# Seven products for the output stages of three middle blocks, on a ring of 2048 tokens, with other places for the folds

## The chip, the core and the metric

The kernel runs on one core of one Trainium2 chip. Its time is device time in microseconds (us), the median of repeated runs. The core's engines are called PE (TensorE, matmuls; PEld its weight loads), DVE (VectorE), ACT (ScalarE), POOL (GpSimd) and SP (SyncE, which issues DMAs). Each engine runs its own instructions in program order and waits for the others through semaphores.

## What is computed

Two stages follow one another: attention over pooled keys and values, then a feed-forward layer whose hidden value is the largest of three products. Cut to the lines that matter:

```python
# q, k, v: (8 batches, 8 heads, 576 tokens, 64)
k_p = k.reshape(B, H, 72, 8, 64).mean(axis=3)      # every 8 keys into one
v_p = v.reshape(B, H, 72, 8, 64).mean(axis=3)
attn = softmax(q @ k_p.T / sqrt(64))
x = (attn @ v_p).transpose(0, 2, 1, 3).reshape(4608, 512)
h = max(max(x @ w1, x @ w2), x @ w3)               # 512 -> 768
out = h @ w_out                                    # 768 -> 512
```

## The kernel before

**Blocks.** The 4608 tokens are worked through in nine blocks of 512, numbered 0 to 8. A block has a hidden stage (`hidden`, L364) and an output stage (`project`, L382). The attention of the coming batches (576 tokens each, so the borders of batches and blocks don't agree) is woven into the matmuls of these stages by hand: a block's list gives, for a numbered slot in the stream of matmul groups, the steps that are issued there (`block` L499, `plan1` L523, `plan` L533). The steps (`do`, L278) are k (transpose the folded keys into `pkt` and copy them into `kz`: two copies on DVE, two on ACT, L198), q or T (transpose q, on PE or by DMA), s0 to s7 (scores of a head into `psc`, exponential into `et` on ACT), v0 to v4 (values of 128 tokens into `pav`; reciprocal and product `xn` on DVE, L261 and L263), x0 to x4 (transpose `xn` into `xT`, on PE up to batch 2 and by a DMA transpose on SP's queue behind it).

**Hidden stage.** The weights w2 and w3 have w1 subtracted, so that h = x w1 + max(0, x(w2-w1), x(w3-w1)). For each of six column groups jc, one group of four matmuls (L347) gives `pw1`, which ACT turns into `t` (L353), and a second gives `pw2`; DVE writes hT = max(t, pw2) (L355). `pw` has three PSUM buffers. Blocks 0 to 5 do this directly; blocks 6 to 8 (the woven end of the program) use seven products instead of eight (Strassen's scheme, `seven`, L753) for it.

**Output stage.** The part x w1 w_out is taken with a matrix wm = w1 w_out, which block 0 computes (`linear`, L329: four groups of six matmuls L334 into `pw` buffers, copied to `wm` by DVE and ACT in turn, L338). A block's four tiles of 128 tokens each take four matmuls with wm (L392) and six with w_out (L396), 128x512 each, into one PSUM bank, which ACT copies to `osb` (L401) for SP to store. Blocks 7 and 8 do this in seven products as well (`out_seven`, L661): a product is ten 128x256 matmuls (L715). It needs sums of the quarters of [wm; w_out], which POOL makes during the last blocks (`fold_out`, L622, 20 instructions L630), and sums of the quarters of [x, h] (`fold_x`, `fold_h`).

**POOL.** Its queue issues the loads of q, k, v and the weights, and folds the eight keys or values that are averaged: `fold` (L147) is three additions of halves (L151, L152, L154). `pool_work` (L543) puts, at the start of each block, the loads for three batches on, then the folds of two or three tensors. Only batch 1's k is folded by DVE (step K in block 0). Sums of the hidden weights for blocks 6 to 8 (`fold_w`, L572) are DVE work in block 5.

Of the kernel before, what the change touches and what calls it, by code (L numbers as in the profile page):

```python
# [14 lines left out]
def kernel(  # L15
# [129 lines left out]
    xT = const.tile([128, KCH, TOK], F16, name="xT", tag="xT")  # L145

    def fold(e, t, out, dtype=F32):  # L147
        part, n = t.shape[:2]
        f = const.tile([part, n, 4, D], dtype, name="half" if dtype == F32 else "halfh",
                       tag="half" if dtype == F32 else "k16")  # L150
        e.tensor_tensor(out=f, in0=t[:, :, 0:4, :], in1=t[:, :, 4:8, :], op=ALU.add)  # L151
        e.tensor_tensor(out=f[:, :, 0:2, :], in0=f[:, :, 0:2, :], in1=f[:, :, 2:4, :],  # L152
                        op=ALU.add)
        e.tensor_tensor(out=out, in0=f[:, :, 0, :], in1=f[:, :, 1, :], op=ALU.add)  # L154
# [81 lines left out]
    def turn_x(b, c0, keep, xn, tag, evac=nc.scalar.copy):  # L236
        if b > 2:
            g0 = S * b + c0
            nc.sync.dma_start_transpose(
                out=xT[:, :, g0 + keep:g0 + 128],  # L240
                in_=xn.rearrange("p g h d -> p (g h d)")[keep:128])
            return
        pxt = psum([128, KCH, 128], F16, name="pxt", tag=tag[0], bufs=tag[1])
        for kc in range(KCH):
            nc.tensor.transpose(
                pxt[:, kc, :],
                xn[:, kc // 2, 2 * (kc % 2):2 * (kc % 2) + 2, :], identh)
        g0 = S * b + c0
        evac(out=xT[:, :, g0 + keep:g0 + 128], in_=pxt[:, :, keep:128])  # L249
# [28 lines left out]
    def do(b, steps):  # L278
# [3 lines left out]
        for name in steps.split():  # L282
# [16 lines left out]
            elif name[0] == "d":  # L299
                for j in range(2):  # L300
                    sub_w(i, j, j + 1)
            elif name[0] == "z":
# [39 lines left out]
    def hidden_part(n, jc, c0, c1, hT):  # L342
        col = slice(NB * n + c0, NB * n + c1)
        for wi in range(1, 3):
            pw = psum([128, c1 - c0], F32, name=f"pw{wi}", tag="pw", bufs=3)
            for kc in range(KCH):
                mm = nc.tensor.matmul(pw, w_sb[wi][:, kc, bass.ts(jc, 128)],  # L347
                                      xT[:, kc, col],
# [32 lines left out]

    def project(n):  # L382
        hT = hTs[n]
        for mm in range(4):
            m = 4 * n + mm
            last = m == TOK // 128 - 9
            osb = sb3.tile([128, C], F32, name="osb", tag="osb", bufs=5)
            for c in ((slice(0, C // 2), slice(C // 2, C)) if last else (slice(0, C),)):
                tag = PW if len(pools) < 3 else PA if last else PO
                po = psum([128, c.stop - c.start], F32, name="po", tag=tag[0], bufs=tag[1])  # L390
                for kc in range(KCH):
                    nc.tensor.matmul(po, xT[:, kc, bass.ts(m, 128)], wm_sb[:, kc, c],  # L392
                                     start=(kc == 0), stop=False)
# [103 lines left out]
    FOLDS = (2, 3, 4, 5, 6, 7, 8, 10)  # L497

    def block(n, plan, parts, folds=()):  # L499

        for slot, _ in enumerate(part for stage in parts for part in stage(n)):
            if slot == 0 and n > 0:
                pool_work(n, mms[-1])
# [3 lines left out]
            if folds and slot in FOLDS:  # L507
                next(folds.pop(0))

    fold_v(1)  # L510
    block(0, {0: [(0, "v2")], 1: [(0, "v3")], 3: [(0, "x2 x3 w1 v4")], 6: [(0, "x4 d1")], 9: [(0, "w2")], 10: [(0, "d2")], 11: [(0, "w3")], 12: [(0, "w4")], 14: [(0, "w5 z")],
              17: [(1, "K")], 24: [(1, "q0 k")], 25: [(1, "q1")],
              26: [(1, "s0 q2")], 27: [(1, "s1 s2")], 28: [(1, "s3 Q3")],
              29: [(1, "s4 s5")], 30: [(1, "s6 s7")], 31: [(1, "v0")],
              32: [(1, "v1 x0")], 33: [(1, "X1 v2 v3")]}, (hidden, project))
    load_k(3, nc.gpsimd)
    load_v(3, nc.gpsimd)
    load_q(3)
    fold_k(2, nc.gpsimd)
    fold_v(2)  # L520


    def plan1():  # L523
        return {1: [(1, "x2")], 2: [(1, "v4")], 3: [(1, "x3")],
                5: [(1, "x4")],
                6: [(2, "k")], 7: [(2, "q0")], 9: [(2, "q1")], 11: [(2, "q2 s0")],
                12: [(2, "s1 q3")], 13: [(2, "s2")], 14: [(2, "s3")], 15: [(2, "s4"), (3, "T")],
                16: [(2, "s5")], 18: [(2, "s7")],
                19: [(2, "v0")],
                20: [(2, "v1 x0")], 21: [(2, "v2 x1")], 22: [(2, "v3 x2")],  # L530
                23: [(2, "v4 x3")], 24: [(2, "x4"), (4, "T")], 17: [(2, "s6")]}

    def plan(n):  # L533
        b = n + 1
        got = {0: [(b, "k")]}
        got.update({3 + h: [(b, f"s{h}")] for h in range(H)})
        got.update({12 + c: [(b, f"v{c} x{c}")] for c in range(5)})
        got[14 if n == 2 else 13].append((b + 2, "T"))
        return got

    FOLDS_OF = {1: "k3 v3", 2: "k4 v4 k5", 3: "v5 k6 v6", 4: "k7 v7"}

    def pool_work(n, mm):  # L543

        if n + 3 < B:
            if n == 1:
                load_q(4)
            after([load_k(n + 3, nc.gpsimd)], mm)
            load_v(n + 3, nc.gpsimd)
            if n > 1:  # L550
                load_q(n + 3)
        for name in FOLDS_OF.get(n, "").split():
            if name[0] == "k":
                fold_k(int(name[1]), nc.gpsimd)
            else:
                fold_v(int(name[1]))
# [31 lines left out]
    def halves(n):  # L588

        return {i: xT[:, 2 * (i // 2):2 * (i // 2) + 2,  # L590
                      NB * n + HALF * (i % 2):NB * n + HALF * (i % 2) + HALF]
                for i in range(4)}
# [18 lines left out]
    th = {}  # L611

    def out_w(z, r):
# [3 lines left out]
        return wm_sb[:, 2 * j + r, c] if r < 2 else wo_sb[:, JH * j + r - 2, c]  # L617

    def out_s(z):
        return so["S4"][:, 0:5] if z == 4 else so["S123"][:, 5 * z - 5:5 * z]  # L620

    def fold_out():  # L622

        for r in range(5):
            a = [out_w(z, r) for z in range(4)]
            s = [None] + [out_s(z)[:, r] for z in range(1, 5)]
            for out, x, y, op in ((s[1], a[2], a[3], ALU.add), (s[2], s[1], a[0], ALU.subtract),
                                  (s[3], a[0], a[2], ALU.subtract),
                                  (s[4], a[1], s[2], ALU.subtract)):
                after([nc.gpsimd.tensor_tensor(out=out, in0=x, in1=y, op=op)], mms[-1])  # L630
                yield
# [29 lines left out]
    def out_seven(n):  # L661

        o = sb2.tile([128, 2304], F32, name="ob", tag="et")[:, 0:2048].rearrange(
            "p (j m c) -> p j m c", j=2, m=2)
# [3 lines left out]
        def store(e, j, c):  # L668
            for u in range(2):
                b, g = divmod(2 * (4 * n + 2 * j) + u, NG)  # L670
                pair = g + 2 < NG and GS[g + 2] == GS[g] + 4
                for m in range(0, 2, 1 + pair):
# [3 lines left out]
                                in_=o[64 * u:64 * u + 64, j, m:m + 1 + pair, c])  # L676

        def bank(of, m):
            if n < LAST:
                if of not in banks:  # L680
                    if of == "A":
# [13 lines left out]
        def product(i, *ms):  # L695
            for m in ms:
                matmuls(i, m)
# [3 lines left out]
        def matmuls(i, m):  # L701
# [3 lines left out]
            for r in range(5):  # L705
                c = slice(128 * m, 128 * m + 128)
                if isinstance(zb, str):
                    z = int(zb[1]) - 1
                    left = turns(n)[:, z, r, c] if r < 2 else th[n][z][:, r - 2, c]
                else:  # L710
                    at = HALF * (zb % 2) + 128 * m
                    left = (xT[:, 2 * (zb // 2) + r, NB * n + at:NB * n + at + 128] if r < 2
                            else hTs[n][:, JH * (zb // 2) + r - 2, at:at + 128])
                right = out_s(int(za[1]))[:, r] if isinstance(za, str) else out_w(za, r)
# [4 lines left out]
        def evict(i, ms):  # L719
            m, at = ms[0], slice(ms[0], ms[-1] + 1)  # L720

            def copy(j, c):
                nc.scalar.copy(out=o[:, j, at, c], in_=bank("A", m))

            def plus(j, c, of):
                nc.vector.tensor_tensor(out=o[:, j, at, c], in0=o[:, j, at, c],
# [26 lines left out]
    def seven(n):  # L753

        x, banks, done = halves(n), {}, set()
        low = pad[:, 8:10]
# [147 lines left out]
```

## Time and profile before

| | us |
|---|---|
| median of three runs (228.23 to 230.03) | 228.53 |
| span of the profiled execution | 227.0 |
| PE busy in it | 217.5 (96%) |
| POOL busy | 153.5 (68%) |
| DVE busy | 131.5 (58%) |
| ACT busy | 122.1 (54%) |

The page cuts the span into 40 slices, each digit a busy share in tenths:

```profile
PE   7688999999999999999999999999999999999993
...
DVE  3568877038525342634363336388668886798841
...
POOL 7974200999949999999999929930224996994020
PEclk9999999999999999999999999999999999999999
```

PE is full from the third slice to the last but one, and its clock (PEclk) is granted in full throughout. POOL is full from a third to two thirds of the span. In the chain of work that ended last, PE has 70%, DMA 12% and POOL 11% of the span.

In the lines from the trace, the columns are: start in us from the span's start, duration in us, engine, line of the code, operation, output <- inputs, shape, how many instructions are merged, and in brackets the engine's idle time just before and what ended it. In a table by stretch, each engine has its busy time and, in brackets, its number of instructions.

### The profile page before, as it was taken

How to read it: one execution, taken by the hardware profiler on the slowest of the kernel's cores; microseconds unless marked ns; L12 is line 12 of the kernel's file. 1: busy time of each engine (PE TensorE's matmuls, PEld its weight loads, DVE VectorE, ACT ScalarE, POOL GpSimd, SP SyncE). 2: the span in 40 equal slices, each digit the busy share in tenths (PEclk: the TensorE clock that was granted, in tenths of full speed). 3: DMA queues.
4: the chain of work that ended last, by engine and by line, in shares of the span. 5: the costliest groups of instructions: out<-in, count | busy, mean ns of one | idle time of the engine just before them, and what ended most of it. 6: DMA issues, size and time to landing. Idle time of an engine off the chain costs nothing.

```text
span 227.0 us, 4497 instructions
## 1 busy us (share of the span) xinstructions
PE 217.5 (96%) x1716; PEld 137.6 (61%) x1717; DVE 131.5 (58%) x251; ACT 122.1 (54%) x221; POOL 153.5 (68%) x131
## 2 busy tenths in 40 slices
PE   7688999999999999999999999999999999999993
PEld 2377745558656555545554555455677777788882
DVE  3568877038525342634363336388668886798841
ACT  2267524755874578237723872574687446554330
POOL 7974200999949999999999929930224996994020
PEclk9999999999999999999999999999999999999999
DMA  6999999989749999987998699962261544200265
GB/s 160 211 197 197 207 208 208 202 157 229 131 104 183 218 174 210 169 188 131 209 168 196 136 191 185 200 143 56 58 106 36 115 63 90 49 0 0 52 205 164
DMA packets 47413, 33.52 MB, mean 148 GB/s; under 512 B 27104, under 2 KB 42400, under 8 KB 47392
## 3 DMA queue, kind: packets, MB, share of 16 engines
q0 software_dynamic: 16944, 16.98, 46.1%
q1 hardware_dynamic: 30000, 15.87, 32.8%
q10 hardware_dynamic: 448, 0.39, 0.7%
q8 instruction: 13, 0.21, 0.4%
q14 instruction: 8, 0.07, 0.1%
HBM read 34.60 MB, written 9.44 MB: 194 GB/s over the span
## 4 chain that ended last, share of the span: by engine, by line
PE 70%; DMA 12%; POOL 11%; DVE 3%; issue 2%; ACT 0%; POOLq 0%; DVEq 0%; ACTq 0%
PE pw L347 21%; PE po L396 14%; PE po L392 9%; DMA vt<-in_v_dram 8%; PE pA L789 6%; PE psc L207 4%; DMA mw<-in_moe_w_dram 4%; PE pav L255 3%; POOL half L151 3%; PE pC L789 3%; PE oA L715 3%; PE oC L715 2%; POOL half L152 2%; PE pB L789 2%; POOL mw L108 1%
## 5 line engine op out<-in xcount | busy, mean ns | idle before, releaser
L347 PE MATMUL pw<-xT,mw 128*128 128x512 f16 (+1 forms) x336 | 72.8, 348 | 0.3 <-ACT xT L249 0.2
L355 DVE TENSOR_TENSOR hT<-t,pw 128x512 f16<-128x512 f16 (+1 forms) x42 | 25.4, 609 | 34.1 <-ACT et L212 25.9
L347 PEld LDWEIGHTS <-mw 128*128 128x128 f16 x336 | 31.6, 98 | 21.2 <-issue 1.0
L396 PE MATMUL po<-mwo,hT 128*128 128x512 f16 (+1 forms) x174 | 41.0, 371 | 0.0
L212 ACT ACTIVATE et<-psc 72x576 f16<-72x576 f32 (+2 forms) x54 | 35.1, 660 | 6.5 <-PE psc L207 6.4
L151 POOL TENSOR_TENSOR half<-vt 72x2048 f32<-72x2048 f16 x7 | 28.4, 4059 | 14.5 <-DMA vt<-in_v_dram 14.1
L401 ACT COPY osb<-po 128x512 f32<-128x512 f32 (+1 forms) x28 | 16.2, 578 | 35.1 <-PE po L396 31.8
L353 ACT ACTIVATE t<-pw 128x512 f16<-128x512 f32 (+1 forms) x42 | 22.5, 537 | 13.0 <-PE pw L347 11.0
L392 PE MATMUL po<-wm,xT 128*128 128x512 f16 (+1 forms) x116 | 28.9, 371 | 0.1
L263 DVE TENSOR_TENSOR xn<-pav,rcp 128x512 f16<-128x512 f32 x40 | 27.6, 691 | 1.4
L152 POOL TENSOR_TENSOR half<-half 72x1024 f32<-72x1024 f32 (+1 forms) x13 | 27.2, 2095 | 1.0
L396 PEld LDWEIGHTS <-hT 128*128 128x128 f16 x174 | 16.1, 98 | 14.1
L207 PE MATMUL psc<-qT,kz 128*128 128x320 bf16 (+2 forms) x120 | 22.4, 278 | 1.0 <-DVE qT L184 0.9
L151 POOL TENSOR_TENSOR half<-ktFalse 96x1536 f32<-96x1536 f16 x6 | 18.6, 3097 | 4.5 <-DMA ktFalse<-in_k_dram 4.3
L207 PEld LDWEIGHTS <-kz 128*128 128x128 bf16 x143 | 13.1, 98 | 13.3 <-ACT qT L184 1.1
L255 PEld LDWEIGHTS <-et 72*128 72x128 f16 x320 | 15.5, 98 | 7.1 <-issue 0.6
L795 ACT CAST pad<-pA 128x512 f16<-128x512 f32 x27 | 15.5, 587 | 7.2 <-PE pA L789 5.6
L261 DVE RECIPROCAL rcp<-pav 128x8 f32<-128x8 f32 x40 | 8.2, 205 | 19.1 <-PE pav L255 18.8
L255 PE MATMUL pav<-vp,et 72*128 72x65 f16 x320 | 16.9, 194 | 0.3 <-POOL vp L154 0.2
L392 PEld LDWEIGHTS <-xT 128*128 128x128 f16 x116 | 10.5, 98 | 8.2 <-issue 0.2
L769 DVE SCALAR_TENSOR_TENSOR hT<-pad 128x512 f16<-128x512 f16 x18 | 14.4, 812 | 1.7 <-ACT pad L799 1.3
L198 DVE COPY kz<-pkt 64x288 bf16<-64x288 bf16 x18 | 8.7, 481 | 11.5 <-PE pkt L189 11.3
(110 smaller groups left out, 320.2 us busy)
## 6 DMA issues: line engine op xcount, KB each, us to landing
out_dram<-osb SPq DMA_DIRECT2D x54, 128.0 KB, 3.9
ktFalse<-in_k_dram POOLq DMA_DIRECT2D x7, 576.0 KB, 6.6
qb<-in_q_dram POOLq DMA_DIRECT2D x7, 576.0 KB, 13.1
vt<-in_v_dram POOLq DMA_DIRECT2D x7, 576.0 KB, 11.1
mw<-in_moe_w_dram POOLq DMA_DIRECT2D x9, 256.0 KB, 9.4
ktTrue<-in_k_dram SPq DMA_DIRECT2D x3, 384.0 KB, 5.2
out_dram<-ob SPq DMA_DIRECT2D x8, 128.0 KB, 2.6
mwo<-in_moe_w_out_dram POOLq DMA_DIRECT2D x1, 768.0 KB, 13.1
```

Source lines behind the costliest of these rows:

```text
L151: e.tensor_tensor(out=f, in0=t[:, :, 0:4, :], in1=t[:, :, 4:8, :], op=ALU.add)
L152: e.tensor_tensor(out=f[:, :, 0:2, :], in0=f[:, :, 0:2, :], in1=f[:, :, 2:4, :], op=ALU.add)
L207: nc.tensor.matmul(out, kz_all[b % 2][f % 2][:, h, :], qTs[b][:, n + i0:n + i1, 64 * (h % 2):64 * (h % 2) + 64], start=True, stop=True)
L212: nc.scalar.activation(out=out, in_=in_, func=FT.Exp, scale=1.0 / 64.0)
L255: nc.tensor.matmul(pav[:, h // 4, 65 * (h % 4):65 * (h % 4) + 65], ets[b][:, h, c0:c0 + 128], vp_all[:, b, h, :], start=True, stop=True)
L263: nc.vector.tensor_tensor(out=xn, in0=pv[:, :, :, 0:D], in1=rcp.to_broadcast([128, 2, 4, D]), op=ALU.mult)
L347: mm = nc.tensor.matmul(pw, w_sb[wi][:, kc, bass.ts(jc, 128)], xT[:, kc, col], start=(kc == 0), stop=(kc == KCH - 1))
L353: nc.scalar.activation(out=t, in_=pw, func=FT.Relu)
L355: nc.vector.tensor_tensor(out=hT[:, jc, c0:c1], in0=t, in1=pw, op=ALU.max)
L392: nc.tensor.matmul(po, xT[:, kc, bass.ts(m, 128)], wm_sb[:, kc, c], start=(kc == 0), stop=False)
L396: nc.tensor.matmul(po, hT[:, jc, bass.ts(mm, 128)], wo_sb[:, jc, c], start=False, stop=(jc == JCH - 1))
L789: mm = nc.tensor.matmul(p[:, w], a[:, kc, bass.ts(g, 128)], b[:, kc, :], start=(i in FIRST and w + kc == 0), stop=(w + kc == 2), skip_grou ...
```

## The change

- `xT` holds 2048 tokens instead of 4608 and is addressed as a ring (`tokens`). A DMA transpose that crosses the seam is cut in two.
- The output stages of blocks 2, 3 and 4 use `out_seven`: seven products of ten 128x256 matmuls in place of 40 matmuls of 128x512. Product A's results are copied by ACT and products B and C are added by DVE (three additions a block).
- The sums of [wm; w_out] are made early: the rows of w_out by four POOL instructions ahead of POOL's first fold (block 0), the rows of wm by four DVE instructions in block 1 (S). The 20 POOL instructions in the last blocks go.
- Blocks 2 to 4 gain eight DVE sums each: four of tokens (a1 to a4) and four of h (b1 to b4). The weight sums of `fold_w` move from block 5 to blocks 1 to 4 (f).
- The order of blocks 1 to 4 is written as one list (`MIDDLE`), POOL's work included: h is a hidden part, a digit a product of the output stage, F a step of the old output stage, `k5<` a load, `k4+1` one more instruction of the fold of k of batch 4 (`+3`, or `+2` where one is done, ends it). `!` makes POOL's next fold instruction wait for the last sum that DVE was given. In block 2 the step k comes after the second hidden part, in block 4 after the sums a1 to a4.
- `osb` becomes three buffers of two tiles each; the buffers `pad` and `pad4` of the last blocks lie where v and q were loaded.

```diff
-    xT = const.tile([128, KCH, TOK], F16, name="xT", tag="xT")
+    RING = 2048
+    xT = const.tile([128, KCH, RING], F16, name="xT", tag="xT")
+
+    def tokens(t0, t1, k0=0, k1=KCH):
+
+        t0, t1 = t0 % RING, (t1 - 1) % RING + 1
+        assert t0 < t1
+        return xT[:, k0:k1, t0:t1]
...
+        g0 = S * b + c0
         if b > 2:
-            g0 = S * b + c0
-            nc.sync.dma_start_transpose(
-                out=xT[:, :, g0 + keep:g0 + 128],
-                in_=xn.rearrange("p g h d -> p (g h d)")[keep:128])
+            cut = 128 - (g0 + 128) % RING
+            cuts = (keep, cut, 128) if keep < cut < 128 else (keep, 128)
+            for a, z in zip(cuts, cuts[1:]):
+                nc.sync.dma_start_transpose(
+                    out=tokens(g0 + a, g0 + z),
+                    in_=xn.rearrange("p g h d -> p (g h d)")[a:z])
             return
...
+            elif name[0] == "S":
+                next(out_sums, None)
...
-    def plan(n):
-        b = n + 1
-        got = {0: [(b, "k")]}
-        got.update({3 + h: [(b, f"s{h}")] for h in range(H)})
-        got.update({12 + c: [(b, f"v{c} x{c}")] for c in range(5)})
-        got[14 if n == 2 else 13].append((b + 2, "T"))
-        return got
-
-    FOLDS_OF = {1: "k3 v3", 2: "k4 v4 k5", 3: "v5 k6 v6", 4: "k7 v7"}
...
-    def fold_out():
-
-        for r in range(5):
-            a = [out_w(z, r) for z in range(4)]
-            s = [None] + [out_s(z)[:, r] for z in range(1, 5)]
-            for out, x, y, op in ((s[1], a[2], a[3], ALU.add), (s[2], s[1], a[0], ALU.subtract),
-                                  (s[3], a[0], a[2], ALU.subtract),
-                                  (s[4], a[1], s[2], ALU.subtract)):
-                after([nc.gpsimd.tensor_tensor(out=out, in0=x, in1=y, op=op)], mms[-1])
-                yield
+        return so_new[0][:, z - 1]
+
+    def fold_out(e, r0, r1):
+
+        if not so_new:
+            so_new.append(const.tile([128, 4, 5, HALF], F16, name="so", tag="ktTrue"))
+        w = [out_w(z, r0, r1) for z in range(4)]
+        t = [None] + [so_new[0][:, z, r0:r1] for z in range(4)]
+        for out, x, y, op in ((t[1], w[2], w[3], ALU.add), (t[2], t[1], w[0], ALU.subtract),
+                              (t[3], w[0], w[2], ALU.subtract),
+                              (t[4], w[1], t[2], ALU.subtract)):
+            e.tensor_tensor(out=out, in0=x, in1=y, op=op)
+            yield
+
+    out_sums = fold_out(nc.vector, 0, 2)
...
+    def sums_of(n, name):
+
+        t = tt_all[0]
+        h = name[0] == "b"
+        part = t[:, :, 2:5] if h else t[:, :, 0:2]
+        c = ([hTs[n][:, JH * i:JH * i + JH, :] for i in range(2)] if h else
+             [tokens(NB * n, NB * n + NB, 2 * i, 2 * i + 2) for i in range(2)])
+        x = [c[i // 2][:, :, HALF * (i % 2):HALF * (i % 2) + HALF] for i in range(4)]
+        a, b = {"1": (x[1], x[0]), "2": (x[3], part[:, 0]), "3": (x[3], x[1]),
+                "4": (x[2], part[:, 1])}[name[1]]
+        gate[:] = [nc.vector.tensor_tensor(out=part[:, int(name[1]) - 1], in0=a, in1=b,
+                                           op=ALU.subtract)]
...
         def product(i, *ms):
-            for m in ms:
-                matmuls(i, m)
+            if mid:
+                for r in range(5):
+                    for m in ms:
+                        matmuls(i, m, (r,))
+            else:
+                for m in ms:
+                    matmuls(i, m)
             done.update((i, m) for m in ms)
             evict(i, ms)
 
...
+    for _ in fold_out(nc.gpsimd, 2, 5):
+        pass
+    fold_v(1)
...
+    def pool_step(n, name):
+
+        what, b = name[0], int(name[1])
+        if name[2:] == "<":
...
+            op = load()
+            if what == "k":
+                after([op], mms[-1])
...
+        for _ in range(int(name[3:] or 3)):
+            op = next(folding[what, b])
+            for x in held:
+                after([op], x)
+            held.clear()
...
+    MIDDLE = {
+        1: """
+            h q4< k4< v4< k3+3 h 1:x2 h 1:v4 h 1:x3 h h 1:x4 h k h q0 h h q1 h h q2 s0 h s1 q3
+            h s2 h s3 S S h s4 3:T S S h s5 f f h s6 f f
+            F s7 F v0 F v1 x0 F v2 x1 F v3 x2 F v4 x3 F x4 4:T F
+        """,
+        2: """
+            h k5< q5< a1 a3 a2 a4 f ! v3+3 v5< h k h h s0 h s1 h s2 h s3 h s4 h s5 h s6 b1 !
+            k4+1 h s7 h b2 b3 b4 ! k4+2 v4+1
+            1 v0 x0 2 v1 x1 6 7 v2 x2 5:T 5 v3 x3 v4 x4 3 4
+        """,
+        3: """
+            h k k6< q6< v6< h a1 a3 a2 a4 f ! v4+2 h h s0 h s1 h s2 h s3 h s4 b1 ! k5+3 h s5 h s6
+            h s7 h b2 b3 b4 ! v5+1
+            1 v0 x0 2 v1 x1 6:T 6 7 v2 x2 5 v3 x3 v4 x4 3 4
+        """,
+        4: """
+            h k7< q7< v7< a1 a3 a2 a4 f ! v5+2 k h h h s0 h s1 h s2 h s3 h s4 b1 ! k6+3 h s5 h s6
+            h s7 h b2 b3 b4 f ! v6+1
+            1 v0 x0 2 v1 x1 7:T 6 7 v2 x2 5 v3 x3 v4 x4 3 6:k 4 v6+2 k7+3 v7+3
+        """}
+    folds = iter([f for wi in range(1, 3) for f in [fold_w(wi)] * 4])
+
+    def middle(n):
+
+        pieces, outs, out_tiles = hidden(n), None, project(n)
+        for name in MIDDLE[n].split():
+            if name == "h":
+                next(pieces)
+            elif name == "F":
+                next(out_tiles)
+            elif name == "f":
+                next(next(folds))
+            elif name == "!":
+                held[:] = gate
+            elif name.isdigit():
+                outs = outs or out_seven(n)
+                outs(int(name), 0, 1)
+            elif name[0] in "ab":
+                sums_of(n, name)
+            elif name[2:3] in ("<", "+"):
+                pool_step(n, name)
+            else:
+                b, _, step = name.rpartition(":")
+                do(int(b or n + 1), step)
+        assert next(pieces, None) is None
+
+    tt_all.append(const.tile([128, 4, 5, HALF], F16, name="tt", tag="tt"))
+    for n in range(1, 5):
+        middle(n)
+    block(5, LEAD, (hidden,))
+    assert next(folds, None) is None
```

## The prediction

> **What bounds the kernel now.** I read the busy times first, then busy time by block (stretches cut at the first hidden matmul of blocks 2, 3 and 4), then the order in time of the places that the change touches.
>
> ```profile
> PE 217.5 (96%) x1716; PEld 137.6 (61%) x1717; DVE 131.5 (58%) x251; ACT 122.1 (54%) x221; POOL 153.5 (68%) x131
> ```
> ```profile
> core 0: us, PE busy (x) PEld busy (x) DVE busy (x) ACT busy (x) POOL busy (x), PEclk, DMA share, GB/s
> 77.93:100.34 22.41, 22.41 (x149) 11.61 (x148) 9.58 (x18) 11.59 (x20) 21.77 (x13) 1.00 1.04 178
> 100.34:122.73 22.39, 22.39 (x148) 11.59 (x147) 9.58 (x18) 11.60 (x20) 21.75 (x13) 1.00 1.03 184
> 122.73:145.38 22.65, 22.65 (x151) 11.65 (x150) 10.54 (x20) 12.54 (x22) 17.98 (x10) 1.00 0.98 175
> ```
> TensorE has no gap in blocks 2 to 4, at full granted clock: every matmul removed there is gained, and every wait put there is paid. VectorE idles over half of it, but GpSimd is busy for nearly all of blocks 2 and 3, and that matters because of this:
>
> ```profile
> 148.13 1.27 POOL L154 TENSOR_TENSOR vp<-half 72x512 f16<-72x512 f32 x1
> 148.23 1.58 DVE L579 TENSOR_TENSOR sw<-mw 128x768 f16<-128x768 f16 x1
> ...
> 201.63 0.89 DVE L646 TENSOR_TENSOR th<-hT 128x512 f16<-128x512 f16 x1
> 202.20 1.65 POOL L646 TENSOR_TENSOR th<-hT 128x256 f16<-128x256 f16 x2
> 202.56 0.78 DVE L646 TENSOR_TENSOR th<-hT,th 128x512 f16<-128x512 f16 x1
> ```
> A VectorE sum of two SBUF tiles takes 0.55 us at 768 columns (L570) when GpSimd is idle. Dispatched 0.10 us into a fold of 1.27 it took 1.58: it ended 0.41 after the fold (149.40). In the second group the two 512-column sums (0.42 alone) and GpSimd's pieces take turns: the second sum waited for the piece queued before it. Instructions with one PSUM operand do not suffer: L355 and L263 stay at 0.69.
>
> **Removed and added on TensorE.** The output stage of block 2 runs from 90.39 to 100.34 = 9.95 us, of which five groups of values take 5 x 0.26; the 40 matmuls are 8.64 (0.216 each). A product of ten 128x256 matmuls, as the last blocks already run it, went from 200.09 to 201.18 = 1.09; seven are 7.63. Gain 1.01 a block, 3.0 in three blocks; a block without stalls is 21.41.
>
> **Block 0: part of the new sums of w_out on GpSimd.** Four 128x768 sums now stand ahead of GpSimd's first fold.
>
> ```profile
> 16.31 0.82 POOL L129 DMA_DIRECT2D mwo<-in_moe_w_out_dram  x1 [0.60 <-DMA mw<-in_moe_w_dram]
> 39.78 4.05 POOL L151 TENSOR_TENSOR half<-vt 72x2048 f32<-72x2048 f16 x1 [14.05 <-DMA vt<-in_v_dram]
> ```
> ```profile
> 31.92 4.70 PE L334 MATMUL pm<-mwo,w1T 128*128 128x512 f16 x21
> 33.09 0.95 DVE L151 TENSOR_TENSOR halfh<-ktFalse 96x1536 f16<-96x1536 f16 x1 [0.20 <-DMA ktFalse<-in_k_dram]
> 34.07 0.56 DVE L152 TENSOR_TENSOR halfh<-halfh 96x768 f16<-96x768 f16 x1
> 34.66 0.35 DVE L154 TENSOR_TENSOR kp<-halfh 96x384 bf16<-96x384 f16 x1
> 34.94 0.68 DVE L338 CAST wm<-pm 128x512 f16<-128x512 f32 x1
> 36.45 0.44 PE L182 MATMUL pqt<-ident,qb 128*128 128x128 bf16 x5
> ```
> GpSimd itself has room: it idles for 14 us until v of batch 1 lands. But w_out lands 13.1 us after its issue at 16.31 (the table of DMA issues), at 29.4. A GpSimd sum of 256 columns takes 0.67 (L599), and its folds grow by 1.9 ns a column (4.06 for 2048, 3.10 for 1536), so 768 columns are about 1.63, estimated from these rows; the four fill 29.5 to 36. VectorE's fold of k comes at 33.09, in the third. Taking turns: first step 34.45 to 35.3, GpSimd's fourth to 36.95, second step to 37.4, third to 37.75, then the first wm copy to 38.4, where it ended at 35.62. L334's fourth group takes that copy's bank (three buffers). It began at 31.92 + 18 x 0.216 = 35.81, so it now starts at 38.45: +2.65. TensorE's later waits for GpSimd, 0.16 at 47.66 and 0.15 at 55.85, vanish in this: **+2.34**. If VectorE, once in, ran its three steps through, it would be 1.2 - 0.3 = +0.9; if a 768-column sum took 3 x 0.63, +3.2. I take turns, as rows 201.63 to 202.56 show.
>
> **s0 waits for keys.**
>
> ```profile
> 79.13 0.97 DVE L198 COPY kz<-pkt 64x288 bf16<-64x288 bf16 x2 [2.78 <-PE pkt L189]
> 80.13 0.69 DVE L355 TENSOR_TENSOR hT<-t,pw 128x512 f16<-128x512 f16 x1
> 80.19 0.97 ACT L198 COPY kz<-pkt 64x288 bf16<-64x288 bf16 x2 [0.60 <-DVE kz L198]
> 81.52 0.41 PE L207 MATMUL psc<-qT,kz 128*128 128x320 bf16 x2
> ```
> VectorE's two kz copies, then ScalarE's two, end 0.36 before s0. In block 2 the keys now come after the second hidden part, so VectorE does hT (0.61, from 2.0 us into the block) before kz: the chain ends at 4.6, against s0's second matmul at 3.73: +0.95. In block 4 the four token sums (1.47, as L599 at 162.65 to 164.12) and a weight sum (0.47) stand ahead of kz, themselves behind the previous block's last addition: again about +0.95. In block 3 the keys keep their place.
>
> **Sums against folds.** Each block adds to VectorE four token sums (1.47), four sums of h (0.55, then 0.47 each: 1.95) and three additions from PSUM (L726, 0.69): 5.5 us, in 12 idle ones. The weight sums moved from block 5 fit likewise. What costs is the order. The next fold starts only behind a sum, but a sum still waits for the fold that runs.
> Block 2 (us from its start, 0.95 included): b1 at 12.1 to 12.6, one fold of k4 (3.1) to 15.7; b2, ready at 14.3, waits 1.4, and b4 ends at 17.2. Products 6 and 7 still find their sums, but VectorE is late with xn of v0, v1, v2, and v4, which needs one of two value banks, waits 0.49.
> Block 3: b1 ends at 9.45, then all of k5's fold (3.1 + 1.8 + 1.0) to 15.5 against b2 at 13.3. In turns b2 ends at 14.95, GpSimd's last step 15.95, b4 16.9 instead of 14.8: v2, v3, v4 wait 0.5 + 0.1 + 0.6.
> Block 4: the same with k6, and a weight sum behind b4: 0.93 + 0.1 + 0.59.
> Block 3's first hidden part also needs the piece of x2 before the ring's seam: xn of v2 at 19.4, SP's transpose queue (1.2 each) and 2.4 to landing put it 0.3 late.
> Against 22.41, 22.39 and 22.65: block 2 is 21.41 + 0.95 + 0.49 = 22.85, **+0.44**; block 3 21.41 + 0.3 + 1.2 = 22.9, **+0.5**; block 4 21.41 + 0.13 (keys of 6) + 0.95 + 1.62 = 24.1, **+1.45**.
>
> The longest fold that this trace shows holding a sum is 1.27 us. The Trainium skill, "SBUF — State Buffer", section "SBUF: two separate sides", says that the shared port pair is held for a whole instruction and that the other engine fully blocks, for VectorE instructions with two SBUF inputs too. By that the folds of 3.1 block whole and the sum stays; capping each wait at 1.2 us instead would take about 0.5 off.
>
> **At nothing.** Ring addresses (the slots overwritten belong to blocks long done); two products' banks (copies of 0.59 fit between products of A, but for some 0.1 before product 3); the gates as such: values are ready 4 us or more before v0; SP's stores, as many bytes. Without that cover, v0 would wait for the fold. The last blocks lose GpSimd's 20 weight sums, but TensorE idles only 0.2 between 158.35 and 222.9, so -0.2 to 0; the tail from 223 to 227 stays.
>
> **Sum**: 2.34 + 0.44 + 0.5 + 1.45 = +4.7; span 227.0 to 231.7. The median of the runs is 1.53 above that span: **233.2 us**.
>
> **Rivals.** *The gain comes through* (faster): VectorE's waits stay inside TensorE's buffers (the bank that hT frees is needed only two hidden parts, 2.2 us, later), and w_out's sums are done before 33. Then -3.0, and 225.5. It needs w_out to land by 26.5; the row says 29.4. 0.15.
> *VectorE is not made to take turns*: a waiting sum gets in and its successors follow. Block 0 +0.9, block 2 +0.44, block 3 -0.5, block 4 +0.35: +1.2, 229.7. For it: no row shows two independent sums against a queued fold. 0.22, with mixtures of these.
> *GpSimd becomes the bound*: it has 13.6 us of folds a block behind two gates; a fold late by more than those 4 us holds v0. 0.03, above 236.
>
> **Numbers.** My case has 0.60 and runs from 231 (one of the s0 waits or block 0 halved) to 236 (long sums in block 0, longer turns). The range 227.2 to 236.0 leaves out the first rival and the last. About 1% (2.3 us) is what a measurement of this kernel can tell: faster 0.15, within 0.22, slower 0.63.
>
> **What would show it.** TensorE idle before L334's (now L348's) fourth group near 36, released by VectorE, and VectorE's k fold stretched from 1.9 to over 4; s0 of blocks 2 and 4 waiting for ScalarE's kz; b2 of each block longer than 1 us beside a k fold; v4 waiting for xn. If the k fold keeps its 1.9 us, or blocks 2 to 4 come at 21.5, I am wrong.

## The result and the profile after

The changed kernel takes 239.69 us (median of four runs, 238.72 to 241.79) against 229.28 for the kernel before in the same comparison. The ratio is 1.047, 95% interval 1.0405 to 1.0535: slower by 10.4 us, where the prediction said 233.2, at most 236.0. The profiled execution has a span of 237.5, 10.5 more than the 227.0 of before. In the sections below a median counts all executions, and a ratio leaves out those more than 1.5% above the fastest of the same kernel, whatever slowed them: of e3_order one in six and of e5_safe three in six (233 to 251 us at a granted clock of 0.951 to 0.991, and no trace shows why), of e1_early two in four, of b0_only one in four, of e4_keys two in twelve.

Lines keep the columns used above; L535 and L544 are now weight sums, L596 the sums of w_out and wm, L611 those of tokens and h, L161 to L164 a fold.

First the table by block, cut at the first hidden matmul of blocks 2, 3, 4 and 5:

```profile
core 0: us, PE busy (x) PEld busy (x) DVE busy (x) ACT busy (x) POOL busy (x), PEclk, DMA share, GB/s
86.09:109.32 23.23, 21.97 (x179) 14.43 (x178) 14.12 (x26) 12.07 (x21) 18.61 (x10) 1.00 0.72 130
109.32:131.65 22.33, 21.82 (x178) 14.39 (x179) 16.39 (x30) 11.61 (x20) 17.31 (x10) 1.00 0.99 187
131.65:155.91 24.26, 22.47 (x183) 14.38 (x181) 17.59 (x33) 11.49 (x20) 18.15 (x10) 1.00 0.90 161
```

Before, the three stretches had 67.45 us with PE full. Now they have 69.82, and PE is idle for 3.56 of it. So blocks 2 to 4 lost 2.4, as predicted to a tenth. But block 2 begins at 86.09 instead of 77.93: 8.2 of the 10.5 us are gone before the first block with seven products. The timeline has two gaps there. In block 0, PE (the last line), VectorE and GpSimd:

```profile
32.72 2.35 POOL L596 TENSOR_TENSOR so<-mwo 128x768 f16<-128x768 f16 x1
33.60 1.88 DVE L162 TENSOR_TENSOR halfh<-halfh 96x768 f16<-96x768 f16 x1
35.02 1.94 POOL L596 TENSOR_TENSOR so<-mwo,so 128x768 f16<-128x768 f16 x1
37.83 0.81 PE L348 MATMUL pm<-mwo,w1T 128*128 128x512 f16 x3 [2.40 <-DVE wm L352]
```

VectorE's step of 33.60 ends 0.41 after the GpSimd sum before it, and the next GpSimd sum 1.48 after that step: they take turns. The step has 1.88 instead of 0.56, and PE waits 2.40. Then block 1:

```profile
66.97 0.77 POOL L100 DMA_DIRECT2D qb<-in_q_dram  x1 [4.23 <-DMA qT<-qb]
...
68.46 4.21 DVE L535 TENSOR_TENSOR sw<-sw,mw 128x768 f16<-128x768 f16 x1
...
69.14 3.10 POOL L161 TENSOR_TENSOR half<-ktFalse 96x1536 f32<-96x1536 f16 x1
...
72.70 2.04 DVE L535 TENSOR_TENSOR sw<-mw,sw 128x768 f16<-128x768 f16 x1
...
75.64 0.61 PE L258 MATMUL pxt<-identh,xn 128*128 128x128 f16 x4 [3.86 <-DVE xn L275]
```

The third of block 1's weight sums (L535) takes 4.21 us instead of 0.55 beside the fold of k of batch 3, the fourth 2.04 beside its second step. VectorE's reciprocal and xn of v0 and v1 are queued behind them, and PE waits 3.86 for the first xn. The table by stretch shows what follows the gap; PEclk is the third number from the end:

```profile
76.00:82.00 6.00, 6.00 (x38) 3.12 (x36) 1.53 (x4) 1.76 (x3) 0.00 (x0) 0.54 0.74 142
82.00:87.00 5.00, 5.00 (x37) 2.52 (x36) 3.48 (x8) 2.62 (x5) 0.00 (x0) 1.00 0.36 80
```

For 6 us the granted clock is 0.54. By that, 6 x (1 - 0.54) = 2.8 us more went there. The stage from 68.94 to 86.09 has 17.15 where it had 10.38 (67.55 to 77.93): +6.8 = 3.86 + 2.8 and small change. The prediction had nothing for this stage.

### The profile page after: what moved, and what is told of

Its sections match the earlier page's. It is cut to its first block, busy times and chain, and to the rows that moved or that the text cites. A ratio compares the mean times of both kernels' runs of the same rounds, so it can differ in the third digit from the quotient of the medians.

```text
span 237.5 us, 4691 instructions
## 1 busy us (share of the span) xinstructions
PE 219.5 (92%) x1806; PEld 147.5 (62%) x1807; DVE 157.4 (66%) x288; ACT 122.2 (51%) x221; POOL 147.8 (62%) x115
## 4 chain that ended last, share of the span: by engine, by line
PE 65%; DVE 17%; DMA 9%; ACT 4%; issue 3%; POOL 1%; DVEq 0%; SPq 0%; ACTq 0%; POOLq 0%
PE pw L361 20%; PE po L415 9%; PE pA L788 7%; PE po L411 5%; PE oA L712 5%; DVE tt L611 4%; PE psc L217 4%; DMA vt<-in_v_dram 3%; PE pC L788 3%; DMA out_dram<-osb 3%; DVE sw L535 3%; PE pav L267 3%; DVE xn L275 2%; PE oC L712 2%; DVE hT L369 2%
## 5 line engine op out<-in xcount | busy, mean ns | idle before, releaser
L161 POOL TENSOR_TENSOR half<-vt 72x2048 f32<-72x2048 f16 x7 | 28.6, 4088 | 4.1 <-issue 2.0
L162 POOL TENSOR_TENSOR half<-half 72x1024 f32<-72x1024 f32 (+1 forms) x13 | 27.7, 2133 | 3.3 <-DVE rcp L273 1.5
L217 PE MATMUL psc<-qT,kz 128*128 128x320 bf16 (+2 forms) x120 | 22.9, 278 | 2.8 <-ACT kz L208 1.8
L415 PE MATMUL po<-mwo,hT 128*128 128x512 f16 (+1 forms) x102 | 24.8, 381 | 0.0
L161 POOL TENSOR_TENSOR half<-ktFalse 96x1536 f32<-96x1536 f16 x6 | 18.6, 3092 | 5.8 <-issue 5.7
L563 POOL TENSOR_TENSOR pad<-xT 128x256 f16<-128x256 f16 x8 | 6.0, 744 | 23.4 <-ACT pad L794 14.8
L267 PE MATMUL pav<-vp,et 72*128 72x65 f16 x320 | 17.4, 196 | 1.9 <-DVE xn L275 1.7
L722 ACT COPY osb<-oA 128x512 f32<-128x512 f32 x12 | 7.0, 586 | 21.0 <-PE oA L712 21.0
L411 PE MATMUL po<-wm,xT 128*128 128x512 f16 (+1 forms) x68 | 17.5, 381 | 0.0
L420 ACT COPY osb<-po 128x512 f32<-128x512 f32 (+1 forms) x16 | 9.2, 573 | 13.3 <-PE po L415 13.3
L415 PEld LDWEIGHTS <-hT 128*128 128x128 f16 x102 | 10.0, 101 | 8.3 <-issue 1.1
L788 PEld LDWEIGHTS <-sw 128*128 128x128 f16 x144 | 13.7, 98 | 2.4
```

The source lines that it names most:

```text
L161: yield e.tensor_tensor(out=f, in0=t[:, :, 0:4, :], in1=t[:, :, 4:8, :], op=ALU.add)
L162: yield e.tensor_tensor(out=f[:, :, 0:2, :], in0=f[:, :, 0:2, :], in1=f[:, :, 2:4, :], op=ALU.add)
L217: nc.tensor.matmul(out, kz_all[b % 2][f % 2][:, h, :], qTs[b][:, n + i0:n + i1, 64 * (h % 2):64 * (h % 2) + 64], start=True, stop=True)
L267: nc.tensor.matmul(pav[:, h // 4, 65 * (h % 4):65 * (h % 4) + 65], ets[b][:, h, c0:c0 + 128], vp_all[:, b, h, :], start=True, stop=True)
L411: nc.tensor.matmul(po, tokens(128 * m, 128 * m + 128)[:, kc], wm_sb[:, kc, c], start=(kc == 0), stop=False)
L415: nc.tensor.matmul(po, hT[:, jc, bass.ts(mm, 128)], wo_sb[:, jc, c], start=False, stop=(jc == JCH - 1))
```

## The experiments

Theory A: block 1's loss is two weight sums against one fold, with the clock behind it; block 0's delay carried them into it; blocks 2 to 4 lose by keys and by folds beside sums. The rivals are in each expectation.

**e1_early.** Block 1's last two weight sums earlier:

```diff
-            h s2 h s3 S S h s4 3:T S S h s5 f f h s6 f f
+            h s2 h s3 S S h s4 3:T S S h s5 f f f f h s6
```

> The last two weight sums of block 1 stand ahead of the sixth score group's hT instead of behind s6, so ahead of GpSimd's fold of k of batch 3. Theory (these two sums waited for that fold, which made v0 and v1 late by 3.9 us, and the granted clock of 0.54 after that gap cost some 2.8 us more): block 1's output stage comes back by 6.8 us, the idle time before the first v group is under 0.3, the clock has no step down, and the time is 232.9 (1.6% above before). Rival (the clock would have dropped, or v0 would have been late, through something else): 239 to 240, as the changed kernel. Between them, only the wait goes: 236.

Measured: 240.84 (237.5 to 242.55), ratio 1.0427 [1.0367, 1.0486]. No gain; the theory's number missed. The timeline shows the same collision one place on:

```profile
69.43 4.03 DVE L535 TENSOR_TENSOR sw<-sw,mw 128x768 f16<-128x768 f16 x1
...
76.18 0.61 PE L415 MATMUL po<-mwo,hT 128*128 128x512 f16 x1 [4.42 <-DVE hT L369]
```

In this execution the clock had already fallen in block 0 (0.51 from 38 to 40 us, behind a gap of 2.33), which put VectorE's sums another 1.6 us later (hT at 65.00 instead of 63.42), while the fold came only 0.8 later (69.93). So the third sum stood before the fold again, and now hT itself was behind it. Moving the sums ahead of one hT (0.7 us) is no cure if what they must stay clear of does not move with them.

**warm17.** Seventeen unused matmuls ahead of x0 in block 1:

```diff
-            F s7 F v0 F v1 x0 F v2 x1 F v3 x2 F v4 x3 F x4 4:T F
+            F s7 F v0 F v1 D x0 F v2 x1 F v3 x2 F v4 x3 F x4 4:T F
...
+            elif name == "D":
+                keep = psum([128, 512], F32, name="keep", tag=TR[0], bufs=TR[1])
+                for _ in range(17):
+                    nc.tensor.matmul(keep, warm[:, 0:128], warm, start=True, stop=True)
```

> The changed kernel with 17 matmuls on the constant of ones (3.7 us) put in front of block 1's x0, where TensorE idles 3.86; their result is not used. They leave the wait as it is. Theory (the idle time is what lowered the clock to 0.54 from 76 to 82 us): clock 1.00 throughout, 2.8 us less than the changed kernel, 236.9. Rival (the clock fell for another reason, such as the load): 239.7 or more.

Measured: 244.87 (239.78 to 246.05). The experiment missed its aim: in the profiled execution, too, the clock fell in block 0, the gap (4.50) moved ahead of the dummy matmuls to hT, and they added 3.7 us behind it. On its own question, whether the idle time lowered the clock, it says nothing.

**fold_last.** GpSimd's fold of k of batch 3 waits for the fourth weight sum; nothing else differs from the changed kernel:

```diff
-            h q4< k4< v4< k3+3 h 1:x2 ...
-            h s2 h s3 S S h s4 3:T S S h s5 f f h s6 f f
+            h q4< k4< v4< h 1:x2 ...
+            h s2 h s3 S S h s4 3:T S S h s5 f f h s6 f f ! k3+3
...
+        if wi == 1:
+            gate[:] = [last]
```

> The changed kernel with one difference: GpSimd's fold of k of batch 3 waits for the fourth of block 1's weight sums; the gap of 2.4 us in block 0 stays. Theory (fold against sums is all that block 1 lost): 6.8 us less than the changed kernel, 232.9, or up to 235.7 in executions where block 0's gap lowers the clock. Rival (the later fold makes block 2's keys or values late): 236 or more.

Measured: 233.69 (232.74 to 234.51), ratio 1.0192 [1.0142, 1.0242]. The two sums and the fold in its timeline:

```profile
69.88 0.55 DVE L535 TENSOR_TENSOR sw<-sw,mw 128x768 f16<-128x768 f16 x1
70.46 0.56 DVE L550 TENSOR_TENSOR sw<-mw,sw 128x768 f16<-128x768 f16 x1
71.17 3.08 POOL L161 TENSOR_TENSOR half<-ktFalse 96x1536 f32<-96x1536 f16 x1 [1.33 <-DVE sw L550]
```

The sums have 0.55 each, block 1 has no gap left, and 6.0 of the 10.4 us are back: the collision in block 1 is most of the loss. Block 0's gap stays (2.26), and behind it the clock fell in this execution (0.50 from 40 to 42 us). The two runs at a clock of 1.00 took 232.74 and 233.46, next to the predicted 233.2.

**b0_only and e2_block0.** The four sums of w_out go to VectorE in block 0: alone (b0_only), and together with e1_early's order (e2_block0):

```diff
-    for _ in fold_out(nc.gpsimd, 2, 5):
-        pass
+    out_sums2 = fold_out(nc.vector, 2, 5)
...
-    block(0, {... 14: [(0, "w5 z")], ... 24: [(1, "q0 k")], ...
+    block(0, {... 14: [(0, "w5 z W W")], ... 24: [(1, "q0 k W W")], ...
```

> The changed kernel with one difference: the four sums of w_out's rows in block 0 run on VectorE instead of GpSimd. The two weight sums of block 1 keep their place behind s6, and blocks 2 to 4 their order. Theory (block 0's delay of 1.9 us is what moved these two sums into GpSimd's fold of k of batch 3, whose start hangs on a load and not on TensorE): both mended at once, the two sums take 0.55 each and end before the fold starts near 68.4, and the time is about 231.0, as e2_block0. Rival (the sums meet the fold also without the delay, so their place is at fault): block 0 alone is mended, 237 to 238.

> As e1_early, and the four sums of w_out's rows of block 0 run on VectorE (two behind the fifth weight sum, two behind the fold of k) instead of on GpSimd. Theory (GpSimd's four sums stretch VectorE's fold of k from 1.9 to 4.9 us and make the first wm copy late): 1.9 us less than e1_early, 231.0, and L348's group near 36 without the gap of 2.40. Rival (the four sums fill VectorE at the same place, so that the wm copies or keys come as late): same as e1_early.

Measured: b0_only 234.12 (231.42 to 235.64), ratio 1.0177 [1.0115, 1.0239]; e2_block0 230.95 (230.87 to 231.12), ratio 1.0084 [1.0058, 1.0110]. The latter is the theory's number. In both, block 0's gap is gone. In b0_only the third weight sum now gets through in 0.56, the fourth does not:

```profile
67.43 0.86 POOL L91 DMA_DIRECT2D vt<-in_v_dram  x1
67.51 4.32 DVE L537 TENSOR_TENSOR sw<-mw,sw 128x768 f16<-128x768 f16 x1
68.30 3.11 POOL L161 TENSOR_TENSOR half<-ktFalse 96x1536 f32<-96x1536 f16 x1
...
72.74 0.40 PE L258 MATMUL pxt<-identh,xn 128*128 128x128 f16 x4 [2.59 <-DVE xn L275]
```

So both answers hold in part. The delay of block 0 made the collision whole (3.86 instead of 2.59), but without it the place of the sums is still a race, lost by tenths in this execution (231.9 of span, 2.7 more than e2_block0). With block 0's mend and the earlier place together, all four runs of e2_block0 clear it, by their times; e3_keys, below, has the same blocks 0 and 1 and shows that this is no more than a win by tenths.

**e3_keys and e3_order.** On e2_block0, a new order of blocks 2 to 4; e3_keys has only the first pair and, of the last, the part up to `s0`:

```diff
-            h k5< q5< a1 a3 a2 a4 f ! v3+3 v5< h k h h s0 ...
+            a1 a3 a2 a4 f h k k5< q5< ! v3+3 v5< h h h s0 ...
...
-            ... b1 ! k4+1 h s7 h b2 b3 b4 ! k4+2 v4+1
+            ... b1 h s7 h b2 b3 b4 ! k4+3 v4+1
...
-            ... b1 ! k5+3 h s5 h s6 h s7 h b2 b3 b4 ! v5+1
+            ... b1 ! k5+1 h s5 h s6 h s7 h b2 b3 b4 ! k5+2 v5+1
...
-            h k7< q7< v7< a1 a3 a2 a4 f ! v5+2 k h h h s0 ... b1 ! k6+3 ... b4 f ! v6+1
+            h k k7< q7< v7< h a1 a3 a2 a4 f ! v5+2 h h s0 ... b1 ! k6+1 ... b4 f ! k6+2 v6+1
```

> As e2_block0, with the keys' part alone of the new order in blocks 2 to 4: in blocks 2 and 4 the keys stand before the second hidden part; GpSimd's folds of k keep the changed kernel's places. Theory (s0's wait for the keys, 0.74 in blocks 2 and 4, is one cause and the folds beside b2 to b4 another): 1.5 us less than e2_block0, 229.5. Rivals: the keys are all of it, 227.1 as e3_order; or they are hidden behind the folds, 231.0.

> As e2_block0, with another order in blocks 2 to 4: the keys stand behind the first or second hidden part and ahead of the token sums' use, and the folds of k of the next batch stand behind the fourth sum of the products instead of the first, so that no fold of 3.1 us runs beside the sums b2 to b4. The gain on TensorE itself is untouched. Theory (s0's wait for keys and the v groups' wait for xn are what took the gain of 1.0 a block): blocks 2 to 4 at 21.5 to 21.9, 4 to 5 us less than e2_block0, 226 to 227, about 1% below before. Rival (the folds, later now, make the next block's k or v late): blocks 2 to 4 stay above 22.4, 229 to 232.

Measured: e3_order 227.10 (226.99 to 248.87), ratio 0.9913 [0.9888, 0.9939]. Blocks 2 to 4 take 22.02, 21.71 and 22.41 (cut as above), together 66.14 against 69.96 in e2_block0: 3.8 less; b2 to b4 take 0.55 to 0.56 each, and s0 of blocks 2 to 4 does not wait. Five of ten e3_keys runs took 228.5 to 229.3, about 2.0 less than e2_block0 (expected 1.5), so the keys are about half of what the order gives and the folds the rest. The other five took 232.2 to 235.4. The profiled execution is one of these: the load of q of batch 4 was issued at 65.43 instead of 66.24 and the fold started 0.80 earlier with it, while the fourth weight sum was dispatched at 66.83 in place of 66.81: it met the fold once more (4.30), and PE waited 3.21. That race is what e5_safe means to close.

**e4_keys.** The keys of batch 6 ahead of v3 in block 4:

```diff
-            1 v0 x0 2 v1 x1 7:T 6 7 v2 x2 5 v3 x3 v4 x4 3 6:k 4 v6+2 k7+3 v7+3
+            1 v0 x0 2 v1 x1 7:T 6 7 v2 x2 5 6:k v3 x3 v4 x4 3 4 v6+2 k7+3 v7+3
```

> As e3_order, with block 4's transposes of the keys of batch 6 before v3 instead of behind the product 3. In e3_order they waited 0.41 for a bank that v3 holds, the keys came 0.31 late for block 5, and product 3 waited 0.30 for the copy of the bank it adds to. Theory: 0.5 to 0.9 less than e3_order, 226.2 to 226.6 (1.1 to 1.2% below before). Rival (VectorE's copies of the keys, 0.97, now make v3's and v4's xn late by as much): 227.1 or more.

Measured: 231.91 (229.00 to 237.56), ratio 1.0085 [1.0049, 1.0122]. The rival, and worse than it said. In the profiled execution (229.00, the fastest of twelve, at a clock of 1.00; the median one has 0.985) PE waited 3.21 for the bank of v4 until ScalarE had copied the keys (142.70 to 143.66); these copies came behind VectorE's (from 141.37), and those behind an addition (140.76) that had waited for product 5's copy.

**e5_safe and e6_tail.** On e3_order: fold_last's gate, with all four weight sums of block 1 ahead of it; the third and fourth sums of w_out behind the first and third wm copies (e5_safe). In e6_tail also v2 before product 7 in block 2, the keys of 6 behind product 4, block 5's scores one slot later:

```diff
-            h s2 h s3 S S h s4 3:T S S h s5 f f f f h s6
+            h s2 h s3 S S h s4 3:T S S h s5 f f f f ! k3+3 h s6
...
-            1 v0 x0 2 v1 x1 6 7 v2 x2 5:T 5 v3 x3 v4 x4 3 4
+            1 v0 x0 2 v1 x1 6 v2 x2 7 5:T 5 v3 x3 v4 x4 3 4
...
-            ... 3 6:k 4 v6+2 k7+3 v7+3
+            ... 3 4 6:k v6+2 k7+3 v7+3
```

> As e3_order, with the two places mended at which a VectorE sum of two SBUF tiles can start after GpSimd has taken up a fold: GpSimd's fold of k of batch 3 waits for the fourth weight sum of block 1, and the third and fourth sum of w_out stand behind the first and third wm copies of block 0 instead of beside GpSimd's fold of v of batch 1. Theory (runs differ by 4 us where they lose such a race, as b0_only and e3_keys did): every run within 0.5 us of 227.1, mean granted clock 0.99 or more. Rival (e3_order's races are won already, and the scatter of the others comes from elsewhere): same median, with single runs some per cent longer; or, if the moved w_out sums make wm or the keys late, 227.5 to 228.

> As e5_safe, with what is left of waits in blocks 2 to 5 taken up: v2 and its transposes before product 7 in block 2 (the ring's seam made block 3 wait 0.29), the keys of batch 6 behind product 4 (they waited 0.41 for a bank), and the scores of block 5 one slot later (s0 waited 0.31). Theory: 0.7 to 1.0 less than e5_safe, 226.1 to 226.4. Rival (waits are handed on: the keys, now later by a product, make s0 wait as long, and values of block 5 come late for block 6): 227.1 or more.

Measured: e5_safe 229.86 (226.34 to 251.00), ratio 0.9898 [0.9872, 0.9923] from three of its six runs, 226.34 to 226.82; the theory's "every run" did not hold (see the result). e6_tail 226.27, all four runs within 0.2, ratio 0.9885 [0.9864, 0.9906]: the best version, 1.15% below the kernel before, from the changed kernel's 4.7% above. Four runs are too few to say that it is free of the long executions of e3_order and e5_safe. Little of it is against e5_safe: the seam's wait and the keys' went, but s0 of block 5 waits 0.72 instead of 0.30, as the rival feared, though not at the rival's 227.1. Its table by block, with the columns of the changed kernel's:

```profile
77.01:98.72 21.71, 21.56 (x178) 14.58 (x177) 12.55 (x25) 12.19 (x21) 16.22 (x10) 1.00 0.96 163
98.72:120.47 21.75, 21.59 (x180) 14.59 (x178) 15.89 (x31) 11.61 (x20) 18.50 (x10) 1.00 1.05 194
120.47:142.32 21.85, 21.70 (x183) 14.74 (x181) 15.56 (x32) 11.60 (x20) 16.51 (x10) 1.00 1.16 184
```

The gain on PE is there: 65.31 against 67.45, 0.7 a block.

**nogate.** e5_safe without the gates of blocks 2 to 4:

```diff
-                held[:] = gate
+                held[:] = gate if n == 1 else []
```

> As e5_safe, with the gates of blocks 2 to 4 taken out: GpSimd's folds there start as soon as their data is there and GpSimd comes to them, and not behind a sum of VectorE. Theory (a queued fold takes the port before a sum that is ready, and holds it to its end): the sums of the tokens and of h wait for whole folds, some of the products or values come late, 229 to 234. Rival (the order of GpSimd's queue places the folds well enough): 227.1, as e5_safe.

Measured: 258.99 (257.93 to 260.49), ratio 1.1301 [1.1267, 1.1334]: some 32 us slower than e5_safe's 226.4, far beyond what the theory said. The two pairs of token sums of block 3 in its timeline, and what PE then waited for:

```profile
111.21 4.76 DVE L615 TENSOR_TENSOR tt<-xT 128x512 f16<-128x512 f16 x2
...
115.89 5.24 DVE L615 TENSOR_TENSOR tt<-xT,tt 128x512 f16<-128x512 f16 x2
...
123.05 1.44 PE L363 MATMUL pw<-xT,mw 128*128 128x512 f16 x3 [8.44 <-DVE hT L371]
```

Each pair takes 0.75 to 0.88 alone. With folds queued back to back the sums wait for one fold step after another (GpSimd's steps start at 111.90, 114.35, 115.77 and 118.98, without a break), hT is queued behind the sums, and PE runs dry. Of the 34.1 us between the two profiled spans (258.8 and 224.7), 23.5 are idle time of PE; the other 10.6 are the same 1806 PE instructions taking longer, at a mean clock of 0.946 against 0.999.

**pause9.** e5_safe with nine copies on ScalarE ahead of v0 in block 1:

```diff
-            F s7 F v0 F v1 x0 F v2 x1 F v3 x2 F v4 x3 F x4 4:T F
+            F s7 F D v0 F v1 x0 F v2 x1 F v3 x2 F v4 x3 F x4 4:T F
...
+            elif name == "D":
+                for _ in range(9):
+                    nc.scalar.copy(out=warm, in_=warm)
```

> As e5_safe, with nine copies of the constant of ones onto itself on ScalarE ahead of v0 in block 1, so that TensorE runs out of work there for some 3 to 4 us with nothing else changed. Theory (idle time of that length lowers the granted clock to about half for some us, as after the changed kernel's 3.86): the time rises by the idle time read from the trace and about 2.8 us more, and the clock shows a step down behind the pause. Rival (the clock of the changed kernel fell for another reason): it rises by the idle time alone, clock 1.00.

Measured: 231.38 (229.57 to 232.58), ratio 1.0094 [1.0059, 1.0129]. The pause came in pieces: 1.03, 1.35, 0.56 us and smaller ones. So it was not the pause intended, and neither theory is decided for one of 3.9. The executions at a mean clock of 0.999 or 1.000 took 229.6 to 230.1, which is e5_safe plus 3.4, the pause alone; those at 0.985 took 232.3 to 232.6, two at 0.993 lie between. So some executions of one program lose 2.5 us with the clock and others nothing; no trace of a losing one was kept, so whether the pause is behind it stays open.

## Why the prediction was wrong

**The step that failed** is in the part on sums against folds: "The weight sums moved from block 5 fit likewise." It was costed at nothing by VectorE's idle time. But the prediction's own rule, that a sum waits for the fold that runs, was worked through for b1 to b4 only, and not for these. The two sums behind s6 met the fold of k of batch 3, whose start hangs on q's transpose (row 66.97) and moved by 0.3 us against the kernel before, while PE and VectorE's queue came 1.4 later through block 0. That delay made the collision whole; b0_only shows that without it the place is still a race that can be lost. The collision cost 6.8 us (3.86 idle, about 2.8 of clock), shown by fold_last, which gives 6.0 back with one wait added. Adding 6.8 to the predicted span of 231.7 gives 238.5; the profiled one is 237.5, and block 0 (next) makes up the difference. All the signs that the prediction named did come: block 0's idle time, the stretched fold, s0's wait, b2 over 1 us, v4's wait. What it had no term for was this stage.

**Block 0**: +2.34 predicted. PE was 0.53 earlier than before ahead of the gap and 1.40 later at the keys of batch 2, behind it: 1.93, or 1.4 against the kernel before. They took turns, as derived: VectorE's three steps took 1.29, 1.88 and 1.67, 4.9 us from first start to last end where 4.66 was derived, and the fourth group came 2.55 late (37.83 against 31.39 + 18 x 0.216) where 2.65 was. What was mis-sized, by 0.4 to 0.9, is what comes before and after it.

**Blocks 2, 3, 4**: 22.85, 22.9 and 24.1 predicted, 23.23, 22.33 and 24.26 measured; sums 69.85 and 69.82. The wait for the piece of x2 before the seam ends with block 3's first matmul, so the table by block counts it to block 2. The last product's six matmuls start at 108.27 and take 0.65, so block 3 could have begun at 108.92 instead of 109.32: 0.40, against 0.3. With that moved, blocks 2 and 3 have 22.83 and 22.73, so the parts are right and not only their sum. These rows show block 2:

```profile
90.76 0.28 PE L217 MATMUL psc<-qT,kz 128*128 128x256 bf16 x1 [0.73 <-ACT kz L208]
...
98.86 3.08 POOL L161 TENSOR_TENSOR half<-ktFalse 96x1536 f32<-96x1536 f16 x1 [1.45 <-issue]
100.50 1.86 DVE L611 TENSOR_TENSOR tt<-hT,tt 128x768 f16<-128x768 f16 x1
```

s0's second matmul starts 4.67 us into block 2 instead of 3.72 in e3_order: 0.95, as predicted (though the prediction's own 4.6 less 3.73 is 0.87); the 0.73 in the row is idle time alone. b2 took 1.86 beside a fold and b4 ended 17.2 us into the block, as derived. In block 3 b2 ended at 14.96 (14.95 derived); the values then waited 0.9 instead of 1.2, counted between the starts of their matmuls. In e3_order, where s0 does not wait and b2 has 0.56, the three blocks are 3.7 us shorter than these: these waits, and not the products, took the gain.

**At nothing**: the gates stay at nothing as placed, but nogate shows that they carry the design: 32 us without them. The bank that product 3 adds to costs 0.3 a block in e6_tail (0.15 of it as idle time: two value groups start at 95.71 and take 2 x 0.26, product 3 starts at 96.54), more than the "some 0.1". From block 5 to the end it is 81.59 us where it was 81.62: s0 of block 5 lost 0.30 to its wait for the keys of batch 6, which the prediction did not have, and the rest gained as much, 0.3, where "-0.2 to 0" had been expected.

**The rivals.** "VectorE is not made to take turns" is refuted by the rows of block 0. "The gain comes through" (225.5) asked for w_out's sums out of the way and VectorE's waits inside PE's buffers; with both arranged, e6_tail comes to 226.27. The page named in the prediction, "SBUF — State Buffer" of the Trainium skill, section "SBUF: two separate sides", says the port pair is held for a whole instruction; row 68.46 agrees in that the sum waited to the end of a fold of 3.1 us, where the trace before had shown 1.27.

**The clock.** After the 3.86 us gap the granted clock was 0.54 for 6 us in the profiled execution. "TensorE: Matmul & The Clock Gate" of the Trainium skill, section "Part 1: The HAM clock gate", gives a free-running window of about 3.4 us of idle time for such a step and says that its place varies from run to run. The 3.86 agrees, but shorter gaps lowered the clock too, and there the measurement decides. In the kept traces a clock of about 0.5 within the stream of matmuls comes only with a gap: with 2.26 (fold_last), 2.33 and 4.42 (e1_early), 2.80 and 4.50 (warm17), 3.35 to 8.44 (nogate). It stayed at 1.00 behind 2.40 (the changed kernel, block 0), 2.59 (b0_only) and 3.21 (e3_keys and e4_keys). So length alone does not decide it. What does can be worked out from these traces. Every low stretch lasts 3.41, 6.83 or 10.24 us, and where a trace has several, their starts lie whole multiples of 3.41 apart (nogate: 100.89, 117.96, 152.09 and 172.57), so the clock changes on a grid of 3.41 us. In the cell of the grid before each of the ten falls PE was idle for 2.02 us or more; in the changed kernel, whose clock falls at 74.70, the grid counted back from there cuts block 0's gap of 2.40 into 1.71 and 0.68, and the clock held. What counts, by this reading, is the idle time within one cell, so a gap of some 2 to 3.4 us lowers the clock or not by where it falls. It was read off afterwards, and no run was made to test it; warm17 and pause9, which were to decide on the clock, missed their aim. That the gap in block 1 cost the 2.8 us is supported by fold_last, where this gap is gone and the clock is 1.00 from there on.

## What to carry to other kernels

When work is moved onto VectorE, time that is idle there is not enough: for each instruction with two SBUF inputs, write down which GpSimd instruction runs or is queued then, and whether the two are tied to the same event. If one hangs on a load and the other on TensorE, every delay elsewhere reopens the race, so close it with a wait (GpSimd's fold behind VectorE's last sum cost nothing here and gave 6 us) rather than with a place that happens to fit. And a step costed at nothing deserves the same rule as the steps that were costed.

## What the runs showed of the hardware that was not expected

A fold that waits for nothing holds a VectorE sum up before its own recorded start. The sums dispatched 0.68 (changed kernel), 0.50 (e1_early), 0.79 (b0_only) and 0.78 us (e3_keys) ahead of the fold's record all waited for its end, and each began after GpSimd had started issuing the load that stands ahead of the fold (row 67.43, then 67.51). The load itself is not what holds them: in e2_block0 sums dispatched during such a load at 103.75 and 104.42 kept 0.75 and 0.88 a pair, with the next fold step behind a gate. So a released fold seems to count from the instruction before it. That reading is inferred from these rows, and no run isolates it; a fold whose recorded start is late would look the same.
